# Strassen's algorithm for the first MLP's first products, over two superblocks of 1,024 tokens

## Chip, cores and metric

The kernel runs on one core of a Trainium2 chip. The metric is the device time of one execution in microseconds (us); the median of three executions stands for the kernel.

## What is computed

```python
for c in range(S // 32):                      # chunked attention, 4 x 8 heads, 768 tokens, 64 wide
    k_full = concat(mem_k, k[32*c-16 : 32*c+40])      # 8 memory keys and a window
    v_full = concat(mem_v, v[32*c-16 : 32*c+40])
    a = softmax(q_c @ k_full.T / 8)
    out[c] = a @ v_full
x = out as (3072, 512)
x = ((x @ w_a) * (x @ w_b)) @ w_out           # first MLP, 512 -> 1536 -> 512
h = x @ w_in                                  # second MLP, 512 -> 1024 -> 512
ln = layernorm(h * softmax(h)) * g_ln
result = ln @ w_out2
```

The weights arrive as 64-bit floats and are turned into fp32 on the core with integer and float operations. Every fp32 operand of a large product is split into a high part (rounded to fp32r) and a low part (the rest), and a product takes three matmuls: high by low, low by high, high by high.

## The kernel before

The 3,072 tokens are taken in six blocks of 512. For each block `ab` (line 438 to 440 through `mm3`) makes a 128-column piece f of x @ w_a and of x @ w_b: four pieces of the inner dimension, three matmuls of 512 columns each, so 12 matmuls for A and 12 for B. ScalarE copies A out of PSUM (line 864), VectorE multiplies it with B (`gate`, line 455), ScalarE rounds it (line 458), VectorE takes the low part (`gate_lo`, line 462). One piece later `x2_step` multiplies the gated piece with w_out: four output pieces, 12 matmuls, summed in four PSUM banks (`acc`) over all 12 pieces of f. `x2_out` (lines 482 to 484) copies the four banks out and stores them to DRAM (`x2d`). Block 0 also turns the 12 pieces of the first MLP's weights into high and low parts (`w1_abs` to `w1_lo`, lines 266 to 302), each in one of 12 SBUF slots, where they stay.

Attention comes in 24 groups of 128 tokens. Each has the stages S (64 small score matmuls, line 172), M (maximum and subtraction, VectorE), X (exp, ScalarE), N (sum and reciprocal on VectorE, product on GpSimd, line 203), T (4 transposes, line 213, copied by ScalarE) and V (64 small matmuls, line 237, copied by ScalarE, low part on VectorE). The four groups of the next block run in slots between the matmuls of the current one, from a list `plan`.

In the last block the second MLP's 16 weight blocks are loaded (`w2_load`), turned (the same functions) and kept in freed slots; GpSimd makes their sums (`t2_sums`, lines 402 and 406). The second MLP already uses Strassen's algorithm in the form of Winograd for x @ w_in (line 556), on pairs of 128-token tiles: `product`, `snap` (a ScalarE copy of a PSUM bank that is then added to, line 569) and `add_max`. Its output product is at lines 690 to 692. `h_load` (line 502) loads a pair's input, `h_sums` (line 517, GpSimd) and `h_split` (lines 534 and 535) prepare it.

TensorE's instructions go out in the order in which they are written, in all stages. VectorE's and ScalarE's do so in block 0 and, VectorE's alone or both, around the last block and the start of the second MLP; in all other stages a planner orders them, and the DMA issues on SyncE (SP) throughout, by readiness in its own model of time.

## Time and profile before

| | us |
|---|---|
| median of 3 runs (lowest, highest) | 971.98 (971.17, 972.38) |
| the profiled execution, its own time | 972.13 |
| its span, first to last instruction | 970.4 |
| TensorE busy in it | 936.9 (97%) |
| VectorE busy | 512.7 (53%) |
| ScalarE busy | 329.4 (34%) |
| GpSimd busy | 123.4 (13%) |

The span is what the trace covers; the execution's own time is 1.7 us longer. Matmuls overlap in the trace, since a matmul's end is modelled: the distance between two starts, not the duration, is what one matmul takes of the engine.

### The profile page before, as it was taken

What the parts mean: (1) busy time and instruction counts of PE and PEld (TensorE: products, weight loads), DVE (VectorE), ACT (ScalarE), POOL (GpSimd) and SP (SyncE); (2) the same over time, 40 slices, a digit from 0 to 9 for tenths busy, and PEclk for the clock granted to TensorE, in tenths of its full rate; (3) what the DMA queues carried; (4) which work ended last, traced back from release to release, by engine and by line L of the source; (5) the groups of instructions that cost most, each with busy time, mean ns of one, the idle gap of its engine ahead of it and who ended that gap; (6) DMA issues with size and microseconds to landing.
All of it is one profiled execution on the core that took longest, in us unless ns stands there. A gap on an engine that the chain in (4) does not pass through costs nothing.

```text
span 970.4 us, 16305 instructions
## 1 busy us (share of the span) xinstructions
PE 936.9 (97%) x7080; PEld 769.1 (79%) x7080; DVE 512.7 (53%) x842; ACT 329.4 (34%) x471; POOL 123.4 (13%) x115
## 2 busy tenths in 40 slices
PE   4899999999999999999999999999889999999998
PEld 3688877888888888888888888877668888888887
DVE  6999953232322212332322212699788666777661
ACT  3767532112221212121211211544453334444331
POOL 0000000000000000000000100186132222222000
PEclk9999999999999999999999999999999999999999
DMA  9960133111211102111111003521111111110001
GB/s 376 421 255 1 50 114 101 50 50 56 87 50 50 50 28 94 49 53 47 66 50 50 23 1 109 196 86 44 60 49 44 44 44 54 45 44 22 23 33 44
DMA packets 22231, 75.49 MB, mean 78 GB/s; under 512 B 2064, under 2 KB 7440, under 8 KB 20752
## 3 DMA queue, kind: packets, MB, share of 16 engines
q1 hardware_dynamic: 21840, 73.41, 21.1%
q8 instruction: 55, 0.90, 0.4%
q0 software_dynamic: 320, 1.05, 0.3%
q14 instruction: 16, 0.13, 0.0%
HBM read 61.87 MB, written 12.58 MB: 77 GB/s over the span
## 4 chain that ended last, share of the span: by engine, by line
PE 78%; DVE 11%; DMA 5%; issue 3%; ACT 2%; SPq 0%; POOL 0%; DVEq 0%; ACTq 0%
PE psh L556 11%; PE pab L438 11%; PE pab L439 10%; PE pab L440 10%; PE acc L438 5%; PE acc L439 5%; PE acc L440 5%; PE pso L691 5%; PE pso L692 5%; PE pso L690 5%; DMA raw<-w1d_dram 4%; DVE z L295 2%; PE px L237 2%; PE pst L675 2%; DVE z L287 2%
## 5 line engine op out<-in xcount | busy, mean ns | idle before, releaser
L438 PE MATMUL pab<-xh,w 128*128 128x512 f32 (+1 forms) x584 | 230.9, 395 | 1.6 <-ACT xh L255 0.9
L439 PE MATMUL pab<-xl,w 128*128 128x512 f32 (+1 forms) x584 | 226.6, 388 | 0.1
L440 PE MATMUL pab<-xh,w 128*128 128x512 f32 (+1 forms) x584 | 226.5, 388 | 0.0
L455 DVE TENSOR_TENSOR asb<-asb,pab 128x512 f32<-128x512 f32 x72 | 49.3, 685 | 197.6 <-PE pab L440 196.9
L438 PEld LDWEIGHTS pab<-xh,w 128*128 128x128 f32 x584 | 110.1, 188 | 25.2 <-ACT xh L255 1.2
L440 PEld LDWEIGHTS pab<-xh,w 128*128 128x128 f32 x584 | 110.1, 189 | 22.7
L439 PEld LDWEIGHTS pab<-xl,w 128*128 128x128 f32 x584 | 110.2, 189 | 21.7 <-DVE xl L260 0.4
L439 PE MATMUL acc<-gl,w 128*128 128x512 f32 x288 | 114.1, 396 | 4.6 <-DVE gl L462 4.6
L438 PE MATMUL acc<-gh,w 128*128 128x512 f32 x288 | 115.2, 400 | 1.8 <-ACT gh L458 1.8
L440 PE MATMUL acc<-gh,w 128*128 128x512 f32 x288 | 113.6, 394 | 0.0
L556 PE MATMUL psh<-w,x2h 128*128 128x512 f32 x336 | 109.5, 396 | 0.4 <-ACT sgl L569 0.3
L864 ACT COPY asb<-pab 128x512 f32<-128x512 f32 x72 | 42.0, 584 | 161.3 <-PE pab L440 160.8
L458 ACT CAST gh<-asb 128x512 fp32r<-128x512 f32 x72 | 44.7, 621 | 146.6 <-DVE asb L455 146.6
L203 POOL TENSOR_TENSOR E<-E,sm 128x512 f32<-128x512 f32 x18 | 18.8, 1043 | 508.7 <-DVE sm L202 508.7
L691 PE MATMUL pso<-w,ll 128*128 128x512 f32 (+1 forms) x200 | 77.0, 385 | 4.0 <-DVE ll L679 4.0
L690 PE MATMUL pso<-w,lh 128*128 128x512 f32 (+1 forms) x200 | 77.0, 385 | 0.0
L692 PE MATMUL pso<-w,lh 128*128 128x512 f32 (+1 forms) x200 | 76.8, 384 | 0.0
L462 DVE TENSOR_TENSOR gl<-asb,gh 128x512 fp32r<-128x512 f32 x72 | 56.5, 785 | 35.8 <-ACT gh L458 35.8
L556 PEld LDWEIGHTS psh<-w,x2h 128*128 128x128 f32 x336 | 63.1, 188 | 13.8 <-ACT sgl L569 0.7
L439 PEld LDWEIGHTS acc<-gl,w 128*128 128x128 f32 x288 | 54.9, 191 | 17.1 <-DVE gl L462 6.2
L438 PEld LDWEIGHTS acc<-gh,w 128*128 128x128 f32 x288 | 54.8, 190 | 14.0 <-ACT gh L458 2.2
L556 PE MATMUL psh<-w,x2l 128*128 128x512 f32 x168 | 65.4, 390 | 0.0
(88 smaller groups left out, 1178.4 us busy)
## 6 DMA issues: line engine op xcount, KB each, us to landing
raw<-w1d_dram SPq DMA_DIRECT2D x11, 1536.0 KB, 22.8
qk<-qkv_dram SPq DMA_DIRECT2D x20, 640.0 KB, 4.1
v<-qkv_dram SPq DMA_DIRECT2D x20, 512.0 KB, 3.6
x2d<-x2s SPq DMA_DIRECT2D x12, 512.0 KB, 2.7
out_dram<-ot SPq DMA_DIRECT2D x23, 256.0 KB, 2.0
x2r<-x2d SPq DMA_DIRECT2D x10, 512.0 KB, 3.6
raw<-win_dram SPq DMA_DIRECT2D x8, 512.0 KB, 5.5
raw<-wout_dram SPq DMA_DIRECT2D x8, 512.0 KB, 4.3
```

Source lines behind the costliest of these rows:

```text
L237: nc.tensor.matmul(of[r][half:half + 64, p // 2, t], v[rows, c, p, :], at[rows, p, t], start=True, stop=True,)
L438: nc.tensor.matmul(ps, wl, xh, start=first, stop=False)
L439: nc.tensor.matmul(ps, wh, xl, start=False, stop=False)
L440: nc.tensor.matmul(ps, wh, xh, start=False, stop=last)
L455: nc.vector.tensor_tensor(out=a_sb, in0=a_sb, in1=pb, op=ALU.mult)
L458: nc.scalar.copy(gh, a_sb)
L462: nc.vector.tensor_tensor(out=gl, in0=a_sb, in1=gh.bitcast(F32), op=ALU.subtract)
L556: nc.tensor.matmul(ps, x, y, start=(start and k == 0 and i == 0), stop=(stop and k == 1 and i == 2), skip_group_check=True,)
L690: nc.tensor.matmul(po, s["lh"][:, f], wl, start=(f == 0), stop=False)
L691: nc.tensor.matmul(po, s["ll"][:, f], wh, start=False, stop=False)
L692: nc.tensor.matmul(po, s["lh"][:, f], wh, start=False, stop=(f == NF2 - 1))
L864: nc.scalar.copy(a_sb, pa)
```

## The change

Blocks 0 and 1 stay direct. The other 2,048 tokens are two superblocks of 1,024. In each, and for each f, the 512 x 256 matrix [w_a piece, w_b piece] and the 1,024 tokens are cut in two by two, and the eight block products (6 matmuls each) become seven, with sums of weight blocks and of token blocks as operands (Winograd's form). The steps of one f, `s_1` to `s_4`, share three PSUM banks; partial sums are copied out by ScalarE (`snap` of old is `part` here) and added by VectorE.

The weights' sums are made in block 1 (`s1_sums`, `s1_split`) and stored to DRAM (`wsa`, `wsb`), and plain blocks in block 0 (`w1_lo`); a ring of two in SBUF is loaded from there in every step (`ring_load`). The tokens' sums (`t1_sums`, `x1_op`) stand in seven freed weight slots.

The third product runs two steps late as 96 units (`third`) of 6 matmuls: two pieces of f and one output piece of one half; VectorE adds each unit to a sum in SBUF. Eight units are left behind the last step, among the second MLP's first products.

The eight attention groups of both blocks of superblock 0 run in block 1, the eight of superblock 1 in superblock 0, with T six ticks and V seven ticks behind S (a tick is six matmuls). The second MLP's weights are turned in superblock 1 in 38 jobs, up to four in a step, each placed behind the last VectorE instruction of the step so far; parts and sums go to DRAM (`w2s`) and are loaded to their places later (`w2_place`). GpSimd makes no weight sums any more. SBUF areas are laid out once for the whole kernel, and only TensorE is in written order after block 0.

```diff
+    wsa = [dram.tile([P, 4, 2, 256], F32, name=f"wsa{f}") for f in range(NF1)]
+    wsb = [dram.tile([P, 3, 2, 256], F32, name=f"wsb{f}") for f in range(NF1)]
+    w2s = [dram.tile([P, 2, WC], F32, name=f"w2s{i}") for i in range(14 + NF2)]
...
+        for i in range(2):
+            nc.sync.dma_start(wsa[f][:, i], w[:, 0, :, 256 * i:256 * i + 256].bitcast(F32))
+        nc.sync.dma_start(wsb[f][:, 2], w[:, 1, :, 256:512].bitcast(F32))
...
+    def s1_sums(q):
+        s1[q] = Z[:, q % 2 * 2 * WC:][:, 0:2 * WC]
+        w = wslot[q][:, 0:2].bitcast(F32)
+        nc.vector.tensor_tensor(
+            out=s1[q].rearrange("p (a c) -> p a c", a=2), in0=w[:, :, 0], in1=w[:, :, 1],
+            op=ALU.add,
+        )
+        z = s1[q].rearrange("p (i c) -> p i c", i=4)
+        for o, a, b, op in (
+            (3, 2, 3, ALU.add),
+            (2, 0, 2, ALU.subtract),
+            (0, 3, 0, ALU.subtract),
+            (1, 1, 0, ALU.subtract),
+        ):
+            nc.vector.tensor_tensor(out=z[:, o], in0=z[:, a], in1=z[:, b], op=op)
+    def s1_split(q):
+        l = s1.pop(q)
+        h = Z[:, 4 * WC:6 * WC]
+        nc.scalar.copy(h.bitcast(F32R), l)
+        nc.vector.tensor_tensor(out=l.bitcast(F32R), in0=l, in1=h, op=ALU.subtract)
+        for k, t in enumerate((h, l)):
+            t = t.rearrange("p (i c) -> p i c", i=4)
+            nc.sync.dma_start(wsa[q][:, 2:4, k], t[:, 0:4:3])
+            nc.sync.dma_start(wsb[q][:, 0:2, k], t[:, 1:3])
...
+    def ring_load(g, part):
+        if g < NSB * NF1:
+            src = (wsa, wsb)[part][g % NF1]
+            nc.sync.dma_start(
+                ring(g, part).rearrange("p i h k f -> p (i h k f)").bitcast(F32),
+                src.rearrange("p i h c -> p (i h c)"),
+            )
...
+    def t1_sums():
+        a, b = stage(0), stage(1)
+        t1, t2, t4 = (
+            ld_tile(2 * TB, "t").rearrange("d (k t) -> d k t", k=2) for _ in range(3)
+        )
+        for o, p, q in ((t1, b[:, 0:2], a[:, 0:2]), (t2, b[:, 2:4], t1),
+                        (b[:, 0:2], b[:, 2:4], b[:, 0:2]), (t4, a[:, 2:4], t2)):
+            nc.vector.tensor_tensor(out=o, in0=p, in1=q, op=ALU.subtract)
+        xsrc.update({2: t2, 3: t1, 5: b[:, 0:2], 6: t4})
+    def x1_op(i):
+        if i in (2, 3, 5, 6):
+            src = xsrc[i]
+        else:
+            src = stage(i // 4)[:, 2 * (i > 0):2 * (i > 0) + 2]
+        h, l = xop(i)[:, 0], xop(i)[:, 1]
+        nc.scalar.copy(h, src)
+        nc.vector.tensor_tensor(out=l, in0=src, in1=h.bitcast(F32), op=ALU.subtract)
...
+    def s_product(ps, g, part, a, x, start, stop):
+        w = ring(g, part)[:, a]
+        xx = xop(x)
+        for k in range(2):
+            for i, (u, v) in enumerate(((1, 0), (0, 1), (0, 0))):
+                nc.tensor.matmul(
+                    ps, w[:, u, k], xx[:, v, k],
+                    start=(start and k == 0 and i == 0),
+                    stop=(stop and k == 1 and i == 2),
+                    skip_group_check=True,
+                )
...
+    def s_split(g, half, src):
+        h, l = gbuf(g % NF1, half)
+        nc.scalar.copy(h, src)
+        nc.vector.tensor_tensor(out=l, in0=src, in1=h.bitcast(F32), op=ALU.subtract)
+    def s_1(g, bank=None):
+        cur["x"] = s_bank(bank)
+        s_product(cur["x"], g, 0, 0, 0, True, False)
+        nc.scalar.copy(part(g, 0), cur["x"])
+    def s_2(g, bank=None):
+        w = s_bank(bank)
+        s_product(w, g, 0, 1, 1, True, True)
+        cur["last"] = nc.vector.tensor_tensor(out=part(g, 0), in0=w, in1=part(g, 0), op=ALU.add)
+    def s_6(g):
+        s_product(cur["x"], g, 0, 2, 2, False, False)
+        nc.scalar.copy(part(g, 1), cur["x"])
+    def s_7(g):
+        cur["v"] = s_bank()
+        s_product(cur["v"], g, 1, 1, 5, True, False)
+    def s_5(g):
+        s_product(cur["x"], g, 0, 3, 3, False, False)
+        ring_load(g + 2, 0)
+        nc.scalar.copy(part(g, 2), cur["x"])
+        cur["last"] = nc.vector.tensor_tensor(out=part(g, 2), in0=cur["v"], in1=part(g, 2), op=ALU.add)
+    def s_3(g):
+        s_product(cur["x"], g, 1, 0, 4, False, True)
+        cur["last"] = nc.vector.tensor_tensor(out=part(g, 2), in0=cur["x"], in1=part(g, 2), op=ALU.mult)
+        s_split(g, 1, part(g, 2))
+    def s_4(g):
+        s_product(cur["v"], g, 1, 2, 6, False, True)
+        ring_load(g + 2, 1)
+        nc.vector.tensor_tensor(out=part(g, 1), in0=cur["v"], in1=part(g, 1), op=ALU.add)
+        cur["last"] = nc.vector.tensor_tensor(out=part(g, 1), in0=part(g, 0), in1=part(g, 1), op=ALU.mult)
+    def third(u):
+        sb, p, n = u // 48, u // 8 % 6, u % 8
+        half, d = 1 - n // 4, n % 4
+        ps = ps_ab.tile([P, TB], F32, tag=f"ps{u % 2}", name="pab")
+        sl = slice(d * P, (d + 1) * P)
+        for i in range(2):
+            f = 2 * p + i
+            w, t = WO(f), gbuf(f, half)
+            mm3(ps, w[:, 0, sl], w[:, 1, sl], t[0], t[1], i == 0, i == 1)
+        a = held["acc"][half]
+        if p == 5 and sb == NSB - 1:
+            o = (EB[:, 0], EB[:, 1], AT)[next_of("o3", 3)]
+            nc.vector.tensor_tensor(out=o, in0=ps, in1=a[:, d], op=ALU.add)
+            nc.sync.dma_start(x2d[NDIR + 2 * sb + half][:, d], o)
+            return
+        if p == 0:
+            nc.scalar.copy(a[:, d], ps)
+        else:
+            nc.vector.tensor_tensor(out=a[:, d], in0=ps, in1=a[:, d], op=ALU.add)
+        if p == 5 and d == 3:
+            nc.sync.dma_start(x2d[NDIR + 2 * sb + half], a)
...
+    def w2_conv(b, z):
+        raw = held["ld"][b].bitcast(I64)
+        w_abs(raw, z)
+        w_range(z)
+        w_sign(raw, z)
+        w_low(raw)
+        w_add(raw, z)
+    def w2_store(name, z, b):
+        w = held["ld"][b].bitcast(F32R).rearrange("p (h c) -> p h c", h=2)
+        nc.scalar.copy(w[:, 0], z)
+        nc.vector.tensor_tensor(out=w[:, 1], in0=z, in1=w[:, 0].bitcast(F32), op=ALU.subtract)
+        nc.sync.dma_start(w2s[name], w.bitcast(F32))
...
+    def w2_jobs_of():
+        srcs, steps = [], []
+        for k in range(2):
+            for n, (r, c) in enumerate(((k, 0), (k, 1), (k + 2, 0), (k + 2, 1))):
+                srcs.append(win2[r * P:(r + 1) * P, c * WC:(c + 1) * WC])
+                op = {0: 0, 2: 1, 3: 2}.get(n)
+                steps.append(("conv", n, None))
+                if op is not None:
+                    steps.append(("store", n, 2 * op + k))
+            for o, a, b, op in ((0, 1, 0, 3), (1, 3, 1, 5), (3, 3, 0, 4), (2, 2, 3, 6)):
+                steps.append(("sub", (o, a, b), 2 * op + k))
+        for f in range(NF2):
+            srcs.append(wout2[f * P:(f + 1) * P, :])
+            steps.append(("conv", f % 4, None))
+            steps.append(("scale", f % 4, 14 + f))
...
+        def job(kind, n, name):
+            if kind == "conv":
+                if not at:
+                    load()
+                cur["b"] = at.pop(0)
+                w2_conv(cur["b"], w2_z(n))
+                return
+            if kind == "sub":
+                w2_sub(*n)
+                n = n[0]
+                b = next_of("raw", 2)
...
+            if kind == "scale":
+                f = name - 14
+                nc.vector.tensor_scalar_mul(w2_z(n), w2_z(n), gln_sb[:, f:f + 1])
+            if not at and (kind == "scale" or (kind, n) in (("store", 0), ("store", 2), ("sub", 2))):
+                load()
+            w2_store(name, w2_z(n), b)
...
+    def staged(j):
+        if j == 3:
+            x1_op(0)
+            x1_op(1)
+        if j == 7:
+            t1_sums()
+            for i in (2, 5, 3, 4, 6):
+                x1_op(i)
...
+        with tc.issue_after(done.ins):
+            s1_sums(f)
+            s1_split(f)
+        if pend is not None:
+            x2_step(*pend, ms=range(2))
+            tick()
+            x2_step(*pend, ms=range(2, 4))
+            tick()
+        pend = (1, f, gh, gl)
...
+    def later(job):
+        def run():
+            with tc.issue_after(cur["last"].ins):
+                job()
+        return run
...
+    for g in range(NSB * NF1):
+        sb, f = divmod(g, NF1)
+        if g == 0:
+            att_load(q0 + 8)
+            attention(q0 + 8, 26, 12.2)
+        last = sb + 1 < NSB and f == NF1 - 1
+        if last:
+            while events:
+                tick()
+            t1_sums()
+        def renew(i):
+            if last:
+                x1_op(i)
+        if sb == NSB - 1:
+            if f == 0:
+                held["ld"] = [ld_tile(2 * WC, "w2ld") for _ in range(3)]
+            for n in range(4):
+                if jobs:
+                    events.setdefault(clock + 1 + 3 * n, []).append(later(jobs.pop(0)))
+        s_1(g, "ps0" if g == 0 else None)
+        tick()
+        s_2(g, "ps1" if g == 0 else None)
+        tick()
+        renew(0)
+        if g == 0:
+            x2_step(*pend)
+            x2_out(1)
+            sb_buffers()
+        s_6(g)
+        tick()
+        renew(1)
+        s_7(g)
+        tick()
+        renew(2)
+        s_5(g)
+        tick()
+        renew(5)
+        more = g >= 2
+        if more:
+            unit(2)
+        renew(3)
+        s_3(g)
+        tick()
+        if more:
+            unit()
+        renew(4)
+        s_4(g)
+        tick()
+        if more:
+            unit()
+        else:
+            for _ in range(4):
+                tick()
+        s_split(g, 0, part(g, 1))
+        renew(6)
+        if sb == NSB - 1:
+            if f == 3:
+                for n in range(4):
+                    if n % 2 == 0:
+                        x2w = x_tile(n // 2, F32R, "w2x").rearrange("p a c -> p (a c)")
+                    r = x2w[:, n % 2 * 1024:n % 2 * 1024 + 1024]
+                    w2_place(w2_order[n], r)
+            if f >= 5 and f % 2:
+                for n in (f - 5, f - 4):
+                    w2_place(w2_order[4 + n], WO(n).rearrange("p h c -> p (h c)"))
+            if f == 10:
+                h_load(0)
...
+    for n in (8, 9):
+        w2_place(w2_order[4 + n], WO(n).rearrange("p h c -> p (h c)"))
+    wo2_place()
+    unit(2)
     h_p1(0)
-    h_a1(0)
-    h_split(1)
+    unit(2)
+    h_load(1)
+    prepare(1)
+    c = ch[0]
+    w = bank()
+    product(w, 0, 1, 1, True, True)
+    add_max(c["h"][:, 0, 0], w, c.pop("s1"), NEG, c["mx"][:, 0:1])
+    unit(1)
+    product(c["x"], 0, 4, 4, False, False)
+    c["u2"] = snap(1, c["x"])
+    unit(1)
     h_a2(0)
+    unit(2)
```

## Rows read from the trace of the kernel before

**Rows 1.** The page: busy time of TensorE, and the chain that ended last, by engine.
```profile
PE 936.9 (97%) x7080; PEld 769.1 (79%) x7080; DVE 512.7 (53%) x842; ACT 329.4 (34%) x471; POOL 123.4 (13%) x115
...
PE 78%; DVE 11%; DMA 5%; issue 3%; ACT 2%; SPq 0%; POOL 0%; DVEq 0%; ACTq 0%
```

**Rows 2.** Busy time by stretch: block 0, block 2, last block, second MLP's start.
```profile
core 0: us, PE busy (x) PEld busy (x) DVE busy (x) ACT busy (x) POOL busy (x), PEclk, DMA share, GB/s
33.50:142.00 108.50, 106.98 (x793) 86.89 (x794) 97.18 (x97) 68.15 (x69) 2.09 (x2) 1.00 0.36 142
262.00:371.00 109.00, 109.00 (x961) 88.85 (x960) 30.70 (x50) 22.32 (x39) 4.17 (x4) 1.00 0.17 54
589.00:693.20 104.20, 97.83 (x413) 79.05 (x412) 79.11 (x71) 44.39 (x51) 41.84 (x22) 0.97 0.29 101
722.00:800.00 78.00, 73.95 (x345) 61.23 (x344) 57.66 (x133) 29.69 (x47) 20.73 (x23) 0.98 0.14 48
```

**Rows 3.** Timeline of TensorE in block 2: first and last of 15 matmuls (start, duration).
```profile
300.04 0.39 PE L438 MATMUL acc<-gh,w 128*128 128x512 f32 x1
...
303.21 0.39 PE L440 MATMUL pab<-xh,w 128*128 128x512 f32 x1
```

**Rows 4.** TensorE's waits in the last block: total us, times, longest.
```profile
PE acc L439 <- DVE gl L462: 4.6, 4, 2.4
PE acc L438 <- ACT gh L458: 1.8, 1, 1.8
```

**Rows 5.** Timeline of TensorE at the second MLP's first output product.
```profile
722.33 0.39 PE L690 MATMUL pso<-w,lh 128*128 128x512 f32 x1
726.76 0.79 PE L691 MATMUL pso<-w,ll 128*128 128x512 f32 x1 [4.04 <-DVE ll L679]
...
729.88 0.40 PE L692 MATMUL pso<-w,lh 128*128 128x512 f32 x1
```

**Rows 6.** VectorE's groups by shape: busy us, mean ns | idle before.
```profile
L455 DVE TENSOR_TENSOR asb<-asb,pab 128x512 f32<-128x512 f32 x72 | 49.3, 685 | 197.6 <-PE pab L440 196.9
L535 DVE TENSOR_TENSOR x2l<-x2s,x2h 128x1024 fp32r<-128x1024 f32 x12 | 14.7, 1225 | 1.8 <-ACT x2h L534 1.7
L535 DVE TENSOR_TENSOR x2l<-x2r,x2h 128x256 fp32r<-128x256 f32 x12 | 5.0, 420 | 0.0
L279 DVE TENSOR_SCALAR z<-z 128x512 f32<-128x512 f32 x4 | 1.7, 420 | 0.3 <-ACT z L266 0.3
L287 DVE SCALAR_TENSOR_TENSOR z<-raw,z 128x512 int32<-128x512 int32 x1 | 0.7, 685 | 0.0
```

**Rows 7.** Timeline of VectorE in block 0, two instructions back to back.
```profile
51.05 0.68 DVE L455 TENSOR_TENSOR asb<-asb,pab 128x512 f32<-128x512 f32 x1
51.65 1.75 DVE L295 CUSTOM_DVE_ANT_0 z<-raw,z 128x3072 uint16<-128x3072 uint16 x1
```

**Rows 8.** ScalarE's groups by shape, columns as in Rows 6.
```profile
L864 ACT COPY asb<-pab 128x512 f32<-128x512 f32 x72 | 42.0, 584 | 161.3 <-PE pab L440 160.8 <-DVE gl L462 0.5
L534 ACT CAST x2h<-x2s 128x1024 fp32r<-128x1024 f32 x12 | 12.6, 1047 | 0.0
L266 ACT ACTIVATE z<-raw 128x512 f32<-128x512 f32 x4 | 2.7, 668 | 5.0 <-DMA raw<-w1d_dram 5.0
L298 ACT CAST w<-z 128x512 fp32r<-128x512 f32 x1 | 0.6, 617 | 0.6 <-DVE z L379 0.6
```

**Rows 9.** TensorE's group of the second MLP's seven products.
```profile
L556 PE MATMUL psh<-w,x2h 128*128 128x512 f32 x336 | 109.5, 396 | 0.4 <-ACT sgl L569 0.3
```

**Rows 10.** Timeline of an attention group in block 2: S, and GpSimd's last step.
```profile
303.53 0.86 PE L172 MATMUL s<-qk 64*32 64x64 f32 x64
...
308.52 1.04 POOL L203 TENSOR_TENSOR E<-E,sm 128x512 f32<-128x512 f32 x1 [22.91 <-DVE sm L202]
```

**Rows 11.** DMA issues: KB each, median us from issue to landing.
```profile
raw<-win_dram SPq DMA_DIRECT2D x8, 512.0 KB, 5.5
raw<-wout_dram SPq DMA_DIRECT2D x8, 512.0 KB, 4.3
```

**Rows 12.** Timeline of SyncE in block 4 (480 to 589 us).
```profile
538.04 0.62 SPq L502 DMA_DIRECT2D x2r<-x2d  x1
```

More of the change, by code (lines that the diff above doesn't have):

```diff
@@ new lines, in fused_kernel @@
+    pend = None
+    for f in range(NF1):
+        pa = ab(0, f, 0)
+        nc.scalar.copy(G0, pa)
+        if f == 0:
+            w1_low(2)
+        run_slot()
+        pb = ab(0, f, 1)
+        if f + 3 < NF1:
+            w1_abs(f + 3)
+        run_slot(f"{f}a")
+        gh, gl = gate(f, pb)
+        run_slot(f"{f}b")
+        if f + 2 < NF1:
+            w1_add(f + 2)
+            w1_hi(f + 2)
+        gate_lo(gh, gl)
+        if f + 3 < NF1:
+            w1_low(f + 3)
+            w1_range(f + 3)
+        if f + 2 < NF1:
+            w1_lo(f + 2)
+        if f + 3 < NF1:
+            w1_sign(f + 3)
+        run_slot()
+        if pend is not None:
+            x2_step(*pend)
+        pend = (0, f, gh, gl)
+        run_slot()
@@ new lines, in fused_kernel, with tick @@
+    x2_step(*pend)
+    i, j = qs[2:]
+    x2_out(0, nc.scalar.copy)
+    att_P(j)
+    att_S(j)
+    N(i)
+    att_M(j)
+    att_X(j)
+    half = TB // 2
+    pa = ab(1, 0, 0, 0, half)
+    T(i)
+    pb = ab(1, 0, 1, 0, half)
+    N(j)
+    V(i)
+    att_L(i)
+    T(j)
+    V(j)
+    att_L(j)
+    in_order.close()
+    in_order.enter_context(tc.manual_schedule(engines={ENG.PE}))
+    events = {}
+    clock = 0
+    def tick():
+        nonlocal clock
+        for fn in events.pop(clock, []):
+            fn()
+        clock += 1
@@ new lines, in attention @@
+    def attention(q0, first, per, each=None):
+        for j in range(8):
+            qi, b = q0 + j, first + int(j * per)
+            for k, fn in zip((0, 0, 0, 0, 0, 6, 7), stages):
+                events.setdefault(b + k, []).append(lambda fn=fn, qi=qi: fn(qi))
+            if j < 7:
+                events.setdefault(b + 1, []).append(lambda qi=qi: att_load(qi + 1))
+            if each is not None:
+                events.setdefault(b + 8, []).append(lambda j=j: each(j))
+    def staged(j):
[6 more added lines that the diff above has]
+                x1_op(i)
@@ new lines, in fused_kernel @@
+    q0 = 4 * NDIR
+    att_load(q0)
+    attention(q0, 0, 8, staged)
+    pend = None
+    for f in range(NF1):
+        split = half if f == 0 else 0
+        pab = []
+        for w in range(2):
+            ps = ab(1, f, w, split, ps=(pa, pb)[w] if split else None, ks=range(2))
+            tick()
+            pab.append(ab(1, f, w, split, ps=ps, ks=range(2, 4)))
+            if w == 0:
+                nc.scalar.copy(G0, pab[0])
+            tick()
+        gh, gl = gate(f, pab[1])
+        done = gate_lo(gh, gl)
+        with tc.issue_after(done.ins):
+            s1_sums(f)
+            s1_split(f)
+        if pend is not None:
+            x2_step(*pend, ms=range(2))
[3 more added lines that the diff above has]
+        pend = (1, f, gh, gl)
+        if f in (9, 11):
+            ring_load((f - 9) // 2, 0)
+            ring_load((f - 9) // 2, 1)
```

548 lines of the change are left out of this document (212 added, 336 removed).

## The prediction

> **What bounds the kernel now.** I read the page first. It shows TensorE busy for 97% of the span, and TensorE as 78% of the chain that ended last [rows 1]. That is an average, so the stretches come next. In block 2 TensorE is busy for all 109.0 us while VectorE works 30.7; in block 0 VectorE works 97.2 of 108.5 us, and TensorE still stands only 1.5 us; the last block and the second MLP's start are the two with idle time and a granted clock under 1.00 [rows 2]. Then the timeline, because durations overlap: 15 matmuls start between 300.04 and 303.21 us, so one takes 0.2264 us of TensorE [rows 3]. Time goes if there are fewer matmuls, or fewer waits in the two stretches with holes.
>
> The holes, sized. The last block's stretch holds 413 TensorE instructions, all of the 512-column kind, since no attention is left: 413 x 0.2264 = 93.5 us in 104.2 [rows 2], a loss of 10.7 us. Named waits are 6.4 of it, all for the gated piece's two halves [rows 4]; there VectorE and ScalarE, in written order, turn the second MLP's weights. The rest is refilling and a lower clock. At the second MLP's first output product a matmul starts 4.43 us after the one before, 4.2 too late, and the eight starts from 726.76 to 729.88 lie 0.45 us apart [rows 5]: TensorE came out of the wait at 1.2 GHz instead of 2.4, which costs 3.12 - 7 x 0.2264 = 1.5 us more. Together 5.7 us.
>
> **What the change removes.** Per piece f and 1,024 tokens, 48 matmuls for A and B become 42. With 12 pieces and two superblocks 144 go: 144 x 0.2264 = **32.6 us**. The third product keeps its count (a unit is 6 matmuls, 96 units per 2,048 tokens are 576, as before), and so does attention, at (109.0 - 432 x 0.2264) / 4 = 2.8 us per group in block 2. The Strassen shape has the same 512 columns and one weight load per matmul, so the row's price holds. The Trainium skill (TensorE: Matmul & The Clock Gate, section Back-to-back issue gap) gives some 131 ns per 512-column matmul in a sustained stream; by that the saving would be an estimated 18.9 us. The trace does not agree here: 226 ns.
>
> The hole of the last block also goes, **10.7 us**: its matmuls wait for a gated piece made one step earlier, while the units run two steps behind, and the last eight units stand among the second MLP's first products. What comes in its place is priced next.
>
> **What it adds, by stretch.**
>
> Block 0: three stores per piece, no compute. Cost 0; they share the queue with the weight loads, and TensorE waits for neither (1.5 us idle in all, with VectorE busier than anywhere [rows 2]).
>
> Block 1: two gate instructions of 0.69 us, a 1,024-wide sum of 1.23, four quarter sums of 0.42 and a low part of 1.23, 5.5 us of VectorE per piece [rows 6], 66 in all; 11 further 1,024-wide instructions for the tokens' sums and parts, 13.5; eight attention groups at no more than (30.7 - 26 x 0.69) / 4 = 3.2 us, 26. That is 105 us against TensorE's 432 x 0.2264 + 8 x 2.8 = 120, or 88%; block 0 ran at 90% without holes. Attention has less room than before: T stands six ticks behind S, 36 x 0.2264 = 8.15 us. In block 2 the chain from the end of S (303.53 + 0.86) to the end of GpSimd's product (308.52 + 1.04) took 5.2 us [rows 10]. V stands one tick, 1.36 us, behind T, against ScalarE's copy of 0.58. Over 16 groups the bounds are 0 and, with a 1.05 us cast in front of each copy [rows 8], 16 x (1.05 + 0.58 - 1.36) = 4.4. I take **+2**.
>
> Entry into superblock 0: from the last group's V to `s_6`, the first step that needs a token sum, TensorE has 60 matmuls, 13.6 us; the copy, two sums, a cast and a low part take 0.58 + 2 x 1.23 + 1.05 + 1.23 = 5.3. The other four operands follow 1.36 us apart in use and 1.23 apart on VectorE, behind piece 11's 5.5 us of sums. Bounds 0 and 5 (those sums in front); **+2**. The change of superblocks: VectorE gets its usual step plus 11 x 1.23 = 13.5 us, 21 us in a step of 66 x 0.2264 = 14.9; the operands are wanted a step later, so most of it is hidden. Bounds 0 and 6; **+1**.
>
> Every superblock step: VectorE has 11 instructions of 0.69 (five sums or products for A and B, two low parts, four unit sums), 7.6 us of 14.9; ScalarE five of about 0.6. Two ScalarE copies per step stand before a later sum into the same bank, covered by one product (1.36 us): 48 in all. The second MLP has 24 such copies, and there its products waited 0.4 us [rows 9]; so 0.8 from below, and with a 1.05 us cast in front of every one 48 x 0.27 = 13 from above. The nearer row is the same pattern: **+2**.
>
> The weights of the second MLP, in superblock 1: 16 blocks of two cheap and two full passes (2 x 0.42 + 2 x 0.69 = 2.2 us [rows 6]), 22 low parts, 8 differences and 8 scalings at no more than 0.69: 62 us over 38 jobs, 6.5 per step. With 7.6 that fills 14.1 of 14.9 us. Back to back a 512-wide instruction starts the next after 0.60, not 0.69 [rows 7]; so counted the step is 12.4 us, 83%. The Trainium skill (VectorE: DVE Perf Modes, section The DRAIN you can't avoid) says that the next instruction starts only when the pipe is empty; by that the step would be the 14.1. The trace's 0.60 is the exception that a later section of that page makes, for an instruction that nothing holds. The bounds come from two stretches with this work: block 0's 1.5 us in 108.5, and the last block's 10.7 in 104.2 [rows 2], over 9.5 steps or 142 us: 2 and 14.6. The last block is the nearer (the same weights), but units have two steps' grace and GpSimd no longer works beside VectorE (41.8 us there): **+6**.
>
> DMA: the ring's two loads per step wait on SP for `s_5` and `s_4`, and attention's loads, the raw weight blocks and the stores are queued behind them. They are wanted 102 and 90 matmuls later, 23 and 20 us; a load of half the larger one's size lands in 4.3 to 5.5 us [rows 11]. Cost 0; without that cover, a rival.
>
> Second MLP's start: the planner orders VectorE, which before went by hand and was late by 5.7 us. Eight unit sums add 5.5 us to it, 48 unit matmuls 10.9 to TensorE. `h_load(1)` stands behind ten weight loads in the text, but the planner moves loads forward: the last block's input load went out at 538 us, inside block 4 [rows 12]. I keep the hole: **0**, bounds -5.7 and +5.
>
> **Sum.** 970.4 - 32.6 - 10.7 + 2 + 2 + 1 + 2 + 6 + 0 = 940.1 us of span; with the 1.7 around it 941.8, and the profiled execution stood 0.15 above the median: **941.6**.
>
> **Rivals.**
>
> A, VectorE becomes the bound in superblock 1. It goes in order, and the store's low part waits for ScalarE's cast (0.62 [rows 8], say 0.7), the first pass for `w_abs` (0.67). If nothing fills these, 22 x 0.7 + 16 x 0.67 = 26 us, 2.7 per step, lift 14.1 to 16.8 against 14.9: 1.9 x 9.5 = 18 us in place of 6, 953. If some five waits come out at the lower clock, 1.5 each, 961. For it: the last block's waits. Against: the planner may fill the gaps. 950 to 966.
>
> B, the other side: a raw weight block that has not landed holds ScalarE. `w_abs` waits for the block; behind it in ScalarE's queue stand the partial-sum copies, for which TensorE waits. A block is asked for about one job ahead, three ticks or 4.1 us, and some in their own job; landing took 4.3 to 5.5 us [rows 11], with no ring loads beside it. A copy has 1.36 - 0.58 - 0.1 = 0.7 us of slack, and a long wait brings the clock's 1.5. From 941.6 to 972 are 30 us, 1.9 per block over 16 blocks: it decides from 0.7 + 0.4 = 1.1 us of lateness in ScalarE's order if each wait also drops the clock, from 2.6 if none does. At 3 us late each with the clock's loss: 941.6 - 6 + 16 x (3 - 0.7 + 1.5) = 996. Against it: where ScalarE's order is the planner's, blocks 1 to 4, TensorE waits for nothing.
>
> C, the additions are nearly all hidden and the second MLP's hole closes: all lower ends give 970.4 - 43.3 + 2 + 0.8 - 5.7 + 1.5 = 926. 924 to 932.
>
> **Chances.** Forecast (933 to 949) 0.57, A 0.20, B 0.10, C 0.13. Reaching from C's upper part into A, 928 to 962 leaves out 0.05 below and 0.15 above. Within 0.2% of 972 (what a measurement of this kernel can tell from no change) lies only B at its deciding point, 0.02; slower 0.08; faster 0.90.
>
> **What would show it.** Right: 144 fewer full matmuls at 0.226 us; steps of some 15 us in superblock 0 (plus 2.8 per group); VectorE over 80% in superblock 1; no wait for a ring load. A shows as TensorE waiting for VectorE in unit or product lines between superblock 1's start and its tenth step; B as ScalarE idle before `w_abs` for a DMA, with TensorE behind a copy; C as no hole before the first output product. Wrong at the root would be a ring load that TensorE waits for, or a matmul spacing above 0.23 us in the superblocks.

## The result and the profile after

The changed kernel takes 955.79 us (median of four runs, 954.62 to 958.24). The kernel before took 972.17 beside it. The ratio is 0.9837 (95% interval 0.9815 to 0.9859), so the change saves 1.6%. The forecast was 941.6: the sign and the range held, and the time lies 14 us above the forecast. The range held because it was drawn to reach into rival A's (950 to 966); A's mechanism is not what filled it, as the runs below show, so as to the cause that was luck. The profiled execution took 956.56 us with a span of 954.8; the sum forecast a span of 940.1.

First the page, as in [rows 1]: busy time by engine, then the chain that ended last.

```profile
PE 906.4 (95%) x6936; PEld 740.5 (78%) x6936; DVE 656.0 (69%) x1124; ACT 377.3 (40%) x561; POOL 81.0 (8%) x97
...
PE 58%; issue 25%; DVE 12%; ACT 2%; DMA 1%; POOL 1%; SPq 0%; ACTq 0%; POOLq 0%; DVEq 0%
```

TensorE has 6,936 instructions against 7,080, so the 144 matmuls are gone. Its busy share fell from 97% to 95%, so there is more waiting than before. A quarter of the chain is "issue", time for which it names no cause, so the chain alone doesn't say where. The windows (columns as in [rows 2]; PEclk is the granted clock as a share of 2.4 GHz) do. In order: block 0, block 1, steps 1 and 2 of superblock 0, its steps 3 to 11, its step 12, superblock 1, and what follows to the end.

```profile
34.20:143.20 109.00, 107.96 (x824) 87.56 (x824) 97.67 (x98) 68.67 (x69) 2.09 (x2) 1.00 0.61 226
143.20:271.28 128.08, 123.47 (x1644) 100.00 (x1637) 91.63 (x147) 47.06 (x73) 8.43 (x8) 0.99 0.61 202
271.28:298.44 27.16, 22.96 (x97) 17.70 (x96) 17.82 (x25) 9.20 (x15) 0.00 (x0) 1.00 0.73 243
298.44:455.54 157.10, 157.10 (x1651) 127.11 (x1650) 82.06 (x135) 45.32 (x80) 8.96 (x8) 1.00 0.47 157
455.54:471.62 16.08, 15.25 (x67) 12.31 (x66) 15.94 (x19) 9.94 (x14) 0.00 (x0) 1.00 0.52 180
471.62:671.48 199.86, 185.70 (x806) 150.01 (x804) 144.92 (x238) 74.03 (x128) 10.86 (x12) 1.00 0.75 265
671.50:954.80 283.30, 277.04 (x1333) 231.61 (x1331) 182.37 (x421) 108.67 (x163) 49.16 (x60) 0.99 0.14 48
```

Superblock 0's steps 3 to 11 have no idle time. Nine steps of 66 matmuls and eight attention groups make 9 x 66 x 0.2264 + 8 x 2.8 = 156.9 us by the prediction's prices; the trace has 157.10. Superblock 1 has 806 matmuls and no attention: 806 x 0.2264 = 182.5 in 199.86 us, 17.4 lost. Its granted clock is 1.00, and VectorE is busy for 72% of it, not for the over 80% that the prediction named as a sign of being right. Step 12 of superblock 0 loses 16.08 - 66 x 0.2264 = 1.1. Steps 1 and 2 lose 27.16 - 96 x 0.2264 = 5.4.

TensorE's waits in superblock 1 (total us, times, longest) answer to [rows 4]:

```profile
PE acc L481 <- ACT u L501: 7.5, 4, 2.4
PE acc L481 <- ACT G L501: 3.2, 2, 2.3
PE acc L481 <- ACT u L510: 1.5, 2, 0.9
PE pab L644 <- ACT acc L550: 1.5, 1, 1.5
PE pab L644 <- DVE acc L552: 0.3, 1, 0.3
```

These 14.0 us are nearly all for ScalarE (the other 3.4 of the 17.4 stand in no wait: the matmuls around a wait start later than one every 0.2264 us): lines 501 and 510 are the partial-sum copies of `s_1` and `s_6`, line 550 the first copy of a unit's sum. ScalarE is busy only 37% of that time, so something holds it. Its own waits for a DMA from 455 to 660 us, 18 of 34.6 us in all:

```profile
ACT w2ld L578 <- DMA w2s<-w2ld: 11.1, 5, 3.3
ACT EB L283 <- DMA w2ld<-wout_dram: 6.6, 3, 2.6
ACT EB L283 <- DMA w2ld<-win_dram: 6.2, 4, 2.5
ACT AT L283 <- DMA w2ld<-win_dram: 5.5, 1, 5.5
ACT AT L283 <- DMA w2ld<-wout_dram: 2.6, 2, 2.0
ACT w2ld L283 <- DMA w2ld<-win_dram: 2.1, 1, 2.1
```

Line 283 is `w_abs`, which waits for a raw weight block; line 578 is the cast of `w2_store`, which waits for a buffer whose former content is still being stored. One such hold in the timeline, chosen rows of TensorE, SyncE and ScalarE:

```profile
483.30 0.32 SPq L580 DMA_DIRECT2D w2s<-w2ld  x1
...
487.71 0.33 SPq L565 DMA_DIRECT2D w2ld<-win_dram  x1
...
489.24 2.88 PE L481 MATMUL acc<-w 128*128 128x512 f32 x12
...
492.21 0.66 ACT L283 ACTIVATE AT<-w2ld 128x512 f32<-128x512 f32 x1 [5.50 <-DMA w2ld<-win_dram]
492.77 0.65 ACT L286 ACTIVATE w2ld<-w2ld 128x512 int32<-128x512 uint32 x1
493.33 0.57 ACT L501 COPY u<-acc 128x512 f32<-128x512 f32 x1
...
493.95 1.43 PE L481 MATMUL acc<-w 128*128 128x512 f32 x5 [1.83 <-ACT u L501]
```

The store goes out at 483.30, the next load 4.4 us later, and 4.5 us after that `w_abs` runs. The copy of `s_1` stands behind two of the job's instructions, though its sum was complete halfway through the 12 matmuls from 489.24 (`s_1`, then `s_2`); TensorE loses 1.83 us. (12 matmuls in 2.88 us are 11 x 0.2264 + 0.39: the price of [rows 3] holds.)

TensorE's waits in block 1 and the entry:

```profile
PE s L186 <- ACT xs L264: 1.9, 2, 1.0
PE pab L481 <- DVE G L659: 1.9, 1, 1.9
PE px L251 <- ACT AT L229: 1.2, 2, 0.7
PE acc L645 <- DVE gh L665: 1.0, 1, 1.0
PE s L186 <- DVE s L164: 0.9, 1, 0.9
PE acc L481 <- ACT u L519: 0.7, 1, 0.7
PE pab L481 <- ACT u L519: 0.7, 1, 0.7
```

Two places. In block 1, S (line 186) and V (line 251) of attention wait, 4.0 us together: S because its bank is still held by the V before (copied out at line 264) or not yet prepared (line 164). One wait of V, 0.7 us, stood there before the change too. At the entry it is piece 11's gate (lines 659 and 665), and in each of steps 1 and 2 `s_3`, which waits 0.7 us for ScalarE's copy of `s_5`'s sum (line 519), because no unit stands between the two yet. VectorE there, first and last of seven sums and operand parts of the tokens, then the gate:

```profile
265.98 1.22 DVE L434 TENSOR_TENSOR t<-xs 128x1024 f32<-128x1024 f32 x1
...
272.79 1.22 DVE L445 TENSOR_TENSOR w<-t,w 128x1024 fp32r<-128x1024 f32 x1
273.93 0.68 DVE L659 TENSOR_TENSOR G<-G,pab 128x512 f32<-128x512 f32 x1
...
276.80 0.69 DVE L665 TENSOR_TENSOR gh<-G,gh 128x512 fp32r<-128x512 f32 x1
```

The second MLP's first hole, and what TensorE does right after it, timeline as in [rows 5]:

```profile
703.21 1.07 PE L865 MATMUL pst<-ident,acc 128*128 128x128 f32 x8 [3.01 <-DVE r L836]
704.03 2.81 PE L743 MATMUL acc<-w2x,w 128*128 128x512 f32 x6
706.64 4.72 PE L743 MATMUL acc<-w 128*128 128x512 f32 x18
```

### The profile page after: what moved, and what is told of

Read it like the earlier page. It is cut to its first block, busy times and chain, and to the rows that moved or that the text cites. A ratio compares the mean times of both kernels' runs of the same rounds, so it can differ in the third digit from the quotient of the medians.

```text
span 954.8 us, 16795 instructions
## 1 busy us (share of the span) xinstructions
PE 906.4 (95%) x6936; PEld 740.5 (78%) x6936; DVE 656.0 (69%) x1124; ACT 377.3 (40%) x561; POOL 81.0 (8%) x97
## 4 chain that ended last, share of the span: by engine, by line
PE 58%; issue 25%; DVE 12%; ACT 2%; DMA 1%; POOL 1%; SPq 0%; ACTq 0%; POOLq 0%; DVEq 0%
PE acc L743 11%; PE acc L481 11%; PE pab L885 5%; PE pab L883 5%; PE pab L884 5%; PE pab L644 4%; PE pab L645 4%; PE pab L646 4%; PE px L251 2%; PE pst L865 2%; DVE Z L312 2%; DVE Z L304 2%; PE s L186 2%; DMA qkv<-qkv_dram 1%; DVE G L659 1%
## 5 line engine op out<-in xcount | busy, mean ns | idle before, releaser
L481 PE MATMUL acc<-w 128*128 128x512 f32 x978 | 239.7, 393 | 13.0 <-ACT u L501 7.5
L481 PEld LDWEIGHTS acc<-w 128*128 128x128 f32 x978 | 181.4, 188 | 55.1 <-ACT u L501 9.7
L743 PE MATMUL acc<-w 128*128 128x512 f32 x360 | 87.3, 394 | 0.0
L644 PE MATMUL pab<-x,w 128*128 128x512 f32 (+1 forms) x200 | 79.9, 400 | 1.2 <-ACT x L272 0.9
L743 PEld LDWEIGHTS acc<-w 128*128 128x128 f32 x360 | 67.3, 189 | 13.9
L645 PE MATMUL pab<-x,w 128*128 128x512 f32 (+1 forms) x200 | 77.6, 388 | 0.1
L646 PE MATMUL pab<-x,w 128*128 128x512 f32 (+1 forms) x200 | 77.5, 387 | 0.0
L883 PE MATMUL pab<-w 128*128 128x512 f32 (+1 forms) x200 | 76.5, 382 | 0.0
L885 PE MATMUL pab<-w 128*128 128x512 f32 (+1 forms) x200 | 76.3, 381 | 0.0
L884 PE MATMUL pab<-w 128*128 128x512 f32 (+1 forms) x200 | 76.1, 381 | 0.0
L705 POOL TENSOR_TENSOR w2ld<-w2ld 128x256 f32<-128x256 f32 x48 | 45.3, 965 | 308.7 <-PE pab L646 203.6
L552 DVE TENSOR_TENSOR acc<-pab,acc 128x512 f32<-128x512 f32 x72 | 49.3, 688 | 14.0 <-PE pab L646 13.4
L217 POOL TENSOR_TENSOR EB<-EB,sm 128x512 f32<-128x512 f32 x18 | 19.5, 1082 | 424.5 <-DVE sm L216 424.5
L644 PEld LDWEIGHTS pab<-x,w 128*128 128x128 f32 x200 | 38.5, 192 | 9.6 <-ACT x L272 1.2
L646 PEld LDWEIGHTS pab<-x,w 128*128 128x128 f32 x200 | 38.4, 192 | 7.5
L645 PEld LDWEIGHTS pab<-x,w 128*128 128x128 f32 x200 | 38.6, 193 | 7.1 <-DVE x L277 0.4
L885 PEld LDWEIGHTS pab<-w 128*128 128x128 f32 x200 | 37.6, 188 | 7.2
L884 PEld LDWEIGHTS pab<-w 128*128 128x128 f32 x200 | 37.6, 188 | 7.1
L883 PEld LDWEIGHTS pab<-w 128*128 128x128 f32 x200 | 37.6, 188 | 7.0
L644 PE MATMUL pab<-gz,w 128*128 128x512 f32 x96 | 37.8, 394 | 1.2 <-DVE acc L552 1.2
L743 PE MATMUL acc<-w2x,w 128*128 128x512 f32 x144 | 38.8, 406 | 0.0
```

The lines of the kernel that those rows point to most:

```text
L217: (eng or nc.gpsimd).tensor_tensor(out=e, in0=e, in1=sm.to_broadcast([P, H, CK]), op=ALU.mult)
L481: nc.tensor.matmul(ps, w[:, u, k], xx[:, v, k], start=(start and k == 0 and i == 0), stop=(stop and k == 1 and i == 2), skip_group_check=True,
L552: nc.vector.tensor_tensor(out=a[:, d], in0=ps, in1=a[:, d], op=ALU.add)
L644: nc.tensor.matmul(ps, wl, xh, start=first, stop=False)
L645: nc.tensor.matmul(ps, wh, xl, start=False, stop=False)
L646: nc.tensor.matmul(ps, wh, xh, start=False, stop=last)
```

## The experiments

Two theories stood first. H: ScalarE's queue is held by weight jobs that wait for a DMA (rival B's mechanism at a lower price). V: VectorE's passes hold the units (rival A); beside them D, that the ring's loads take the bandwidth. Ratios are to the kernel before, with 95% intervals.

**Deeper buffers.** Six buffers in turn in place of two (two freed token areas hold four), loads three jobs ahead, four placements later. This kernel takes buffers in plain rotation, so it loads some blocks over blocks not yet turned; its work is the same.

```diff
-        b = next_of("raw", 2)
+        b = next_of("raw", 6)
...
-                if not at:
+                for _ in range(3 - len(at)):
                     load()
...
-            if f == 3:
+            if f == 10:
                 for n in range(4):
```

> The changed kernel took 955.8 us; its steps in superblock 1 take 17.8 us more than their matmuls. Theory H (held ScalarE): ScalarE's queue stands at w_abs for a raw weight block that has not landed and at the store's cast for a buffer that is still being stored, with the copies that TensorE waits for behind it. This kernel gives blocks and stores six buffers instead of two and asks for a block three jobs ahead; every compute instruction is kept. By H those waits nearly vanish and some 10 to 12 us go: 943 to 946. Theory V (VectorE is the bound in superblock 1): VectorE has the same work, so 954 to 957. Theory D (the DMA engines are too busy there): the same bytes move, the loads only ask earlier, so 950 to 956.

Measured: 944.65 us, ratio 0.9714 (0.9697 to 0.9732). ScalarE's DMA waits fall from 34.6 to 10.9 us, superblock 1 from 199.86 to 189.78. H stands, with one reservation: a load over a block still in use starts earlier than it may.

**Less VectorE work.** Of every block, the sign and the low word's sum are left out.

```diff
         w_range(z)
-        w_sign(raw, z)
         w_low(raw)
-        w_add(raw, z)
```

> Leaves out two full VectorE passes (sign and low word) per weight block of the second MLP, 32 instructions of 0.6 to 0.7 us or some 21 us of VectorE, so the weights are not right; ScalarE's and the DMA's work is kept. Theory V: most of the 17.8 us of superblock 1 goes, 942 to 948. Theory H: ScalarE is held as before, 952 to 957. Theory D: as H.

Measured: 954.75, ratio 0.9821 (0.9791 to 0.9852). Superblock 1 with 32 VectorE instructions and 19.5 us of VectorE less than after:

```profile
470.81:671.64 200.83, 188.22 (x806) 152.48 (x805) 125.45 (x206) 75.39 (x129) 9.78 (x12) 0.98 0.74 264
```

It takes no less time. TensorE's waits are 12.5 us in place of 14.0, and a stretch of 18 matmuls behind one of them took 5.99 us in place of 4.24 at a lower clock. V falls: VectorE is not the bound. One thing H had not expected: ScalarE's DMA waits fell too, to 20.1 us, so TensorE's loss does not go in step with their sum.

**No ring loads in superblock 1.** Its weight operands are stale; the matmuls stay.

```diff
     def ring_load(g, part):
-        if g < NSB * NF1:
+        if g < NF1 + 2:
```

> Leaves out the ring loads of superblock 1 from its third step on (10 steps of 1.75 MB), so its products use stale weights; all compute work is kept. Theory D: raw blocks and stores land sooner, ScalarE's waits for DMA fall to a third and 8 to 12 us go, 944 to 948. Theory H in its narrow form (two buffers, each of which makes a round trip of load, conversion and store, whatever else the engines carry): a few us at most, 950 to 956.

Measured: 958.39, ratio 0.9854 (0.9834 to 0.9874).

```profile
471.00:673.40 202.40, 188.88 (x806) 152.36 (x804) 144.91 (x238) 74.83 (x129) 10.51 (x12) 0.98 0.49 171
```

The traffic falls from 265 to 171 GB/s, transfers land sooner, and nothing is won: ScalarE's DMA waits fall from 34.6 only to 30.5 us, TensorE's waits from 14.0 to 13.5. D falls: when a transfer may start weighs more than its speed. The time also lies above what H stated here. The trace shows the difference: two stretches of 18 matmuls behind a wait took 6.00 us each in place of 4.24 (shown in the last section).

**Token sums earlier.** On the changed kernel, two sums and one operand are taken at the old place and the rest tied behind the last gate.

```diff
-            t1_sums()
-            for i in (2, 5, 3, 4, 6):
-                x1_op(i)
+            t1_sums(range(2))
+            x1_op(2)
...
         with tc.issue_after(done.ins):
+            if f == NF1 - 1:
+                t1_sums(range(2, 4))
+                for i in (5, 3, 4, 6):
+                    x1_op(i)
             s1_sums(f)
```

> Only the entry into superblock 0 is changed: the last two of the four token sums, and the four operands not wanted first, stand behind block 1's last low part on VectorE instead of in front of its last gate. Theory O (order: the sums delay the last gate, and TensorE waits for it): the first two steps of superblock 0 lose 5.4 us beyond their matmuls now; with this order 1 to 2, so the kernel takes 951 to 953. Rival W (VectorE simply has too much work there, whatever the order): the loss moves to the operands, 955 to 957.

Measured: 962.02, ratio 0.9883 (0.9864 to 0.9901). Both theories missed. Steps 1 and 2 lost 3.7 instead of 5.4, but step 3 now loses 3.2, and superblock 1, with none of its own lines changed, takes 205.21 us for 804 matmuls, 5.8 us more than by the changed kernel's loss. Of these, 2.1 us are longer waits of TensorE (16.1 in place of 14.0), and 3.2 are two stretches of 18 matmuls that took 5.83 and 5.88 us in place of 4.24, at a granted clock of 0.72. ScalarE in step 3:

```profile
299.38 0.62 ACT L498 CAST gz<-u 128x512 fp32r<-128x512 f32 x1 [4.46 <-DMA x2d<-Z]
```

A cast waits for block 1's output to leave the area it writes: one more ScalarE instruction held by a transfer.

**Deeper buffers, each freed only when its job is done**, with a list of free buffers in place of the rotation; the base of the next ones.

```diff
-        b = next_of("raw", 6)
+        b = w2_free.pop(0)
...
             w2_store(name, w2_z(n), b)
+            w2_free.append(b)
```

> The six-buffer version of before loaded some weight blocks into buffers whose block had not been turned yet; this one takes a buffer only when its store or its last use is written. Theory H: the same 944 to 946 (944.7 there), with the steps of superblock 1 behind its first at 15.0 us. If the wrong overlap had hidden part of the wait: 947 to 951.

Measured: 950.34, ratio 0.9775 (0.9762 to 0.9788), in the second of the stated ranges. The free list is the only edit, so part of the first kernel's gain was its loading over blocks in use. Superblock 1 takes 195.34. ScalarE waits for a DMA 10.3 us in all, yet in superblock 1's first step TensorE waits 3.8 us for the copy. ScalarE there:

```profile
471.93 0.67 ACT L283 ACTIVATE EB<-w2ld 128x512 f32<-128x512 f32 x1 [1.33 <-DMA w2ld<-win_dram]
472.50 0.61 ACT L495 CAST g5h<-G 128x512 fp32r<-128x512 f32 x1
473.01 0.66 ACT L286 ACTIVATE w2ld<-w2ld 128x512 int32<-128x512 uint32 x1
473.58 0.65 ACT L283 ACTIVATE EB<-w2ld 128x512 f32<-128x512 f32 x1
474.12 0.64 ACT L286 ACTIVATE w2ld<-w2ld 128x512 int32<-128x512 uint32 x1
...
476.26 0.58 ACT L501 COPY G<-acc 128x512 f32<-128x512 f32 x1
```

`later` ties a job to a VectorE instruction, but its ScalarE passes are not kept there: with their blocks landed early, the planner puts the passes of several jobs in a row ahead of the first copy.

**The entry's edit, the attention's and a later start, each on top of that.** The first moves the sums as above and stages block 1's output in an area of its own; the second runs T and V one tick earlier in block 1; the third starts jobs one step later.

```diff
+        xs = x_tile(2, F32, "x2s") if bi else None
...
+            if bi:
+                t = xs[:, m:m + 2]
```

> Six buffers, and the entry into superblock 0 in the other order, with block 1's output staged in an area of its own instead of the one in which the weights' sums and the gated pieces stand. In the run that only changed the order, the first two steps lost 3.7 instead of 5.4 us, but the third lost 3.2, with ScalarE held for 4.5 us by the store of block 1's output, in whose area a gated piece was to go; and superblock 1 lost more than before. Theory H for the entry too (that store is the cause of the third step's loss): the three steps lose 1 to 3 us instead of 5.9, 940 to 943. Rival W (VectorE has too much work there): 944 to 947.

```diff
-    attention(q0, 0, 8, staged)
+    attention(q0, 0, 8, staged, (5, 6))
```

> Six buffers, and in block 1 the stages T and V of an attention group stand five and six ticks behind S instead of six and seven, so two ticks lie between V and the next group's S. Block 1 loses 4.2 us at attention's stages now, 3.3 of it where S waits for ScalarE's copy of V's bank one tick earlier. Theory: those 3.3 go and T's chain of 5.2 us still fits 6.8: 941 to 943. Rival: T now waits instead, 944 to 947.

```diff
-                if jobs:
+                if jobs and f:
```

> Six buffers, and the 38 jobs start one step later in superblock 1. The changeover's two steps lose 4.7 us in the six-buffer run, 3.6 of it in superblock 1's first, where ScalarE takes the first job's two passes before the cast that frees a buffer for a copy. Theory H: without jobs there 2 to 3 us go, 941.5 to 943. Rival V (VectorE's 21 us of work in that step): the loss stays, 944 to 946.

Measured: 951.14 (0.9779, 0.9765 to 0.9792), 952.57 (0.9795, 0.9777 to 0.9813) and 947.56 (0.9744, 0.9729 to 0.9758). All three lie above both of their stated ranges. The first wins nothing that can be told from its base. The second loses 3.6 in step 2, a copy (line 688 of its kernel) behind a store. Its block 1 is some 1.5 us shorter than its base's, but that is not the edit: block 1 of the first and the third, where T and V are not moved, takes 126.7 us too, and the edit's 126.5. What differs is the granted clock of block 1's first 17 us, 0.90 in the base and 1.00 in these. The third's median is 2.8 under its base's; between the profiled executions it is 2.6, and 1.3 of that is block 1, by the same clock. Its jobs are written a step later, yet the first step of superblock 1 still loses 6.2: from 471.5 to 475.5 us ScalarE runs six conversion passes ahead of its copy. Where a job stands in the text does not decide its place on ScalarE.

**A tie for ScalarE.** A job is tied behind the last partial-sum copy too: first on the deeper buffers, then on the changed kernel with its two buffers.

```diff
-        nc.scalar.copy(part(g, 0), cur["x"])
+        cur["act"] = nc.scalar.copy(part(g, 0), cur["x"])
...
-            with tc.issue_after(cur["last"].ins):
+            with tc.issue_after(cur["last"].ins), tc.issue_after(cur["act"].ins):
                 job()
```

> Six buffers (950.3 us without more), and ScalarE's passes of a job stand behind the step's last partial-sum copy on ScalarE, as VectorE's stand behind its last instruction already. Theory P (placement): the planner moves w_abs and the low-word pass forward, since only VectorE's part of a job is tied to its place; they then stand in front of the copies, and wait there for a block. By P superblock 1's first step loses 1 to 3 us instead of 5.7, and its others at most 2 in all instead of 6.3: 941 to 944. Theory H alone (buffers were all of it): 949 to 951.

> The changed kernel with its two buffers, and only ScalarE's passes tied as in the run beside it. By P alone the placement is enough: superblock 1 loses 5 to 8 us instead of 15.1 behind its first step, 944 to 948. If two buffers cannot feed the jobs in their places whatever the order (H), ScalarE waits for the block at its own place and TensorE still behind it: 951 to 955.

Measured, with six buffers: 940.91, ratio 0.9664 (0.965 to 0.9678), at the lower end of theory P's range. Superblock 1, then ScalarE at its start:

```profile
470.72:655.23 184.51, 182.87 (x806) 150.73 (x804) 144.00 (x238) 74.64 (x130) 9.81 (x12) 1.00 0.79 284
...
473.76 0.59 ACT L501 COPY G<-acc 128x512 f32<-128x512 f32 x1 [0.58 <-DVE g5l L496]
474.24 0.67 ACT L283 ACTIVATE EB<-w2ld 128x512 f32<-128x512 f32 x1
```

The copy now runs ahead of the passes, ScalarE has no wait for a DMA, and the steps from the second to the eleventh take 14.96 us each. Of 17.4 us, 2.0 are left. With two buffers the same tie gives 952.59 (0.9793, 0.9771 to 0.9815), as H stated, and 35.3 us of DMA waits remain:

```profile
470.30:672.57 202.27, 189.15 (x805) 152.23 (x804) 145.38 (x238) 75.10 (x130) 10.64 (x12) 0.98 0.73 262
```

So superblock 1 takes 199.9 us with neither edit, 202.3 with the tie, 195.3 with the buffers, and 184.5 with both. The profiled execution of the tie alone took 957.62 us, 5 more than its median, so its 202.3 is on the high side. TensorE's waits there, which leave out what a lower clock adds, are 14.0, 13.0, 8.6 and 1.6 us; the kernels' medians are 955.79, 952.59, 950.34 and 940.91. (The intervals of the first two just meet.)

**The entry's edit, then the attention's, on the tied kernel.**

> Six buffers, the tied passes, and the entry into superblock 0 in the other order with its own staging area, which alone changed the entry's first two steps from 5.4 to 4.5 us. If the two gains add: 1 us under the run with six buffers and tied passes, 940 to 943. If the planner's new order takes it back: no difference to that run.

> The version of 938.7 us, and attention's T and V in block 1 one tick earlier. In the run with six buffers and that edit block 1 gained some 1.4 us, but the second step of superblock 0 lost 2.6 more, where ScalarE was held for 3.8 us by a store out of the area in which block 1's output was staged. With the staging area of its own that hold cannot come: if it was the cause, 936.5 to 937.7; if the earlier stages cost time by themselves, 938.5 to 941.

Measured: 938.72 (0.9644, 0.9631 to 0.9657) and 936.14 us (935.07 to 937.88; ratio 0.9622, 0.9609 to 0.9635). The last is the fastest version and beats both kernels. The medians fall by 2.2 and 2.6 us, both a little more than was expected, but the intervals of neighbours overlap; only those of the first and the last of the three do not. In the profiled executions most of the first fall is not the edit: block 1 is 1.9 us shorter with the same waits for other engines, at a clock of 1.00 in its first 17 us in place of 0.91. The entry's first two steps are 1.1 shorter (26.12 in place of 27.18 us). In the last, block 1 has no wait of S for a score bank left; in their place T waits for GpSimd's product:

```profile
PE pt L227 <- POOL EB L217: 2.3, 2, 1.6
PE px L251 <- ACT AT L229: 1.3, 3, 0.7
```

## Why the prediction was right, and where it was wrong

Term by term, against the span of 954.8:

- **Matmuls removed, -32.6: right**, in count and in price. The tied kernel's steps of 14.96 us for 66 matmuls are 0.2267 each. The 131 ns of the Trainium skill (TensorE: Matmul & The Clock Gate, section Back-to-back issue gap) show nowhere in this kernel either.
- **The last block's hole, -10.7: gone**; no unit waits for a gated piece. Superblock 1's loss has another cause and is counted there.
- **Block 0's stores, 0: right.** Block 1's first matmul starts at 143.21 us against 142.48 before, 0.7 later, and block 0's first at 34.24 against 33.56 already; block 0 itself takes 108.97 against 108.92.
- **Attention in block 1, +2: mis-sized.** Its waits are 4.0 us, 3.3 of them new, inside the bounds. The forecast mechanism, V waiting for ScalarE's copy of T, is 1.2 of this (0.5 new); S waiting for its bank, 2.8, was not on the list. Another 1.3 is the granted clock, 0.90 in block 1's first 17 us: block 1 takes 128.07 us here and 126.73 in the first run with six buffers, with the same waits at 1.00. Superblock 0's attention cost nothing.
- **Entry, +2: mis-sized**, at 5.4, beyond the upper bound of 5. The bound took piece 11's sums ahead of the operands. What happened is that the planner put seven of the token instructions (1.22 us each) ahead of piece 11's gate; `s_2`'s bank and block 1's last third product then wait for the gate, 1.9 and 1.0 us. Another 1.4 is `s_3` waiting for the copy of `s_5`'s sum in steps 1 and 2. The prediction counted two copies per step, each covered by one product; this third one has the units before it in later steps, and nothing in these two.
- **Partial-sum copies, +2: nothing in superblock 0's steps 3 to 11** (157.10 us against 156.9 without them), and in superblock 1, once nothing holds ScalarE, two waits of 0.8 us.
- **Superblock 1: the step that failed.** Changeover, copies and weights were forecast at 1 + 1 + 6 = 8 and took 1.1 + 17.4 = 18.5. The prediction sized this on VectorE, from the last block's loss, and gave the rest to rival A. VectorE has 144.0 us of work in the 184.5 us of the tied kernel and holds nobody, and taking 19.5 us from it won nothing. Rival B named the mechanism (`w_abs` waits for its block, copies behind it, TensorE behind these) at 0.10. Both of its signs came: ScalarE idle before `w_abs` for a DMA, and TensorE behind a copy; A's sign, TensorE waiting for VectorE, is 0.3 us. B's priced case, 16 blocks of 3 us each with the lower clock, did not come: 18 waits of 1.9 us on the mean, at a clock of 1.00, and 15.4 us of TensorE's time come back when the waits and the order are both mended. Three things of it were not seen: that `w2_store` waits for a buffer in the same way (11.1 of the 34.6 us), that a buffer's round trip through a store and a load takes some 9 us of a 15 us step, and that the planner moves ScalarE's passes ahead of the copies even where no block is late.
- **The argument against B was the error.** In blocks 1 to 4, where ScalarE's order is the planner's, TensorE waited for nothing; but no ScalarE instruction there is a conversion that waits for a DMA (from 153 to 589 us ScalarE waits for TensorE and VectorE alone). That stretch could say nothing about one that does.
- **Ring loads, 0: right.** No matmul waits for one; they land in 5.6 and 5.3 us (medians in superblock 1).
- **Second MLP's start, 0: the hole moved and shrank a little.** TensorE waits 3.0 us instead of 4.2, at the transposes ahead of the first output product and not in it, and the clock falls again: the 24 matmuls from 704.03 us take 1.8 more than at 2.4 GHz, where it was 1.5. From superblock 1's end to the last instruction are 283.3 us with 1,333 TensorE instructions; before, 277.2 held 1,298 from the last block's end. The 35 more are worth 7.9 at 0.2264, and 6.1 was added: 1.8 better, 0.9 of it by the hole.

The differences are +10.5 for superblock 1 and its changeover, +3.4 for the entry, +2.6 for block 1 (3.3 + 1.3 - 2), -1 for superblock 0's copies, +0.7 ahead of block 0 and -1.8: together 14.4. Measured are 14.7. With ScalarE's part repaired the kernel takes 940.9, near the forecast of 941.6, but not by the forecast's way: that sum allows 8 us to superblock 1 and its changeover, where 3.2 are then left, and too little to the entry and block 1.

What stays open: which of the planner's moves made TensorE's waits longer in superblock 1 behind the entry's edit, and why the clock fell behind some waits and not behind others. The version without ring loads is slower than the changed kernel by 2.6 us in the median, but their intervals overlap, and its two stretches at the lower clock are 3.5 us.

## What to carry to other kernels

An engine that goes in order is as late as the latest transfer that any of its instructions waits for, however idle it is: beside busy shares, list for every engine that feeds the bound which of its instructions wait for a DMA, how long a buffer's whole round trip is, and who is queued behind. Before arguing from a quiet stretch, see whether it holds such an instruction at all. A fixed order on the held engine and deeper buffers were worth some 3 and 5 us alone (the 3 at the edge of the noise), and 15 together. A difference of 1 or 2 us between two profiled executions says little before the granted clock of each stretch has been compared.
